# Attention beside an FFT filter: the PV product with V as the stationary operand

## The chip, the cores and the metric

The kernel runs on one core of a Trainium2 chip, in one launch. The metric is the device time of one execution in microseconds. The core's engines are named as the profile names them: PE multiplies matrices (PEld is its loading of the stationary operand), ACT evaluates functions such as exp, DVE works on vectors, POOL sets and copies memory here, and SP issues transfers. PE writes into PSUM, which has eight banks of 128 partitions by 512 f32 columns; the other engines read PSUM and write SBUF. The clock that PE gets is granted by a throttle and stands in the profile.

## The reference

x is 2048 tokens by 448 numbers in bfloat16. Two branches are computed from it and mixed token by token with a gate. A is attention with 16 heads of 28 numbers, B is a filter in the two-dimensional frequency domain.

```python
def reference(A_x, A_wqkv, A_wo, B_x, B_w_r, B_w_i, gate_w):
    # A: q, k, v from x @ wqkv (16 heads of 28)
    scores = einsum("bhqd,bhkd->bhqk", q, k) * 28 ** -0.5
    p = softmax(scores)
    a = (einsum("bhqk,bhkd->bhqd", p, v)).reshape(1, 2048, 448) @ wo
    # B: filter of the same x
    X = rfft2(x, axes=(-2, -1)) * (w_r + 1j * w_i)
    b = irfft2(X, s=(2048, 448), axes=(-2, -1)).astype(bfloat16)
    g = sigmoid((x * gate_w).sum(-1, keepdims=True))
    return g * a + (1 - g) * b
```

## The kernel before

**Layout.** Everything lies in one class, and a scheduler orders the instructions of each engine by the priority at which they were written; what stands between `bg_begin` (L146) and `bg_end` gets a late priority and fills the gaps of the main loop. PSUM is shared out in four parts: `ps_S` (L164) has two buffers of three banks ("psS") for the scores, `ps_pv` (L167) one bank ("pv") for the weighted sums of V, and `ps_bg` (L170) one bank ("bg") for everything in the background.

**Start.** `phase_setup` (L230) issues one transfer of all of x (L236), then the weights, gate and output weights (L243 to L248), all from SP. It transposes x with 64 matmuls against the identity (L257) into xT, 128 features by 2048 tokens in four slices of features. The last slice has 64 rows only; the rows behind are set to zero by POOL (L265, and L267 for the weights) and row 64 to one, so that the weights can add a constant. `fft_setup` (L576) loads the constants of the filter at late priority. Then, for the head tile of the "rep" group and for tile 0, `proj_setup` (L304) copies the weights of each head to columns 32s+1 to 32s+28, and `proj_matmuls` (L337) makes q and k transposed, up to four heads in the four strips of 32 partitions. Row 0 of a strip carries a bias: one in k, and -(|q|^2 + max|k|^2)/2 in q, so that the exponent stays below zero. The norms are matmuls with the selector Sel4 (`proj_knorm`, L361, and `proj_qbias`, L393); the bias row is made in a small tile and moved into q by a transfer on SP. `vproj_and_gate` (L280) makes V for all tokens, 29 columns a head with a one at the end, and the gate.

**Main loop.** `main_loop_group` (L528) runs six groups. The first is one head, replicated in three strips, with its query chunks side by side; the other five hold three heads each. A chunk is up to three heads by 512 queries. For each of 16 key tiles, PE makes three score tiles of 128 keys by 512 queries in three row tiles (L553), ACT takes exp of all 1536 columns (L557) into one of three "Pt" buffers, and PE adds up P V with 12 matmuls (L562):

```python
nc.tensor.matmul(psPV[:, e, j, 0:Dh + 1],
                 lhsT=Pt[:, e, 128 * j:128 * j + 128],
                 rhs=self.vsb[:, i, h, 0:Dh + 1],
                 start=first, stop=last)
```

P is the stationary operand (a load of 128 x 128 for each matmul), V moves with 29 columns, and the result lies by tokens: column 28 of each head is the softmax's denominator. At a chunk's end DVE takes the reciprocal of the denominators, 128 x 12 (L568), and multiplies (L571) into osb, token-major.

**Background.** In this order: `proj_tile` (L426) for tiles 1 to 3; the filter as products with cosine and sine matrices in five steps, `fft_f1` (L605, four matmuls of 450 columns a token tile), `fft_f2` and `fft_f5` (both `_stage_A`, L617, 32 times two matmuls of 256 columns), `fft_f34` (L647, transposes, four matmuls, complex product on DVE) and `fft_f678` (L691); and `tail` (L721), which for each of 16 token tiles transposes osb (L733), copies it (L738, L740), multiplies with Wo (L747), mixes with the filter's result by the gate (L749, "fin") and sends it out (L751). The last four token tiles depend on the last chunk.

Of the kernel before, what the change touches and what calls it, by code (L numbers as in the profile page):

```python
# [16 lines left out]

BG_PRIORITY_BASE = 10_000_000


def bcast_last(ap: bass.AP, n: int) -> bass.AP:
    assert ap.ap[-1][1] == 1
    new_ap = [list(p) for p in ap.ap[:-1]] + [[0, n]]
    return bass.AP(tensor=ap.tensor, offset=ap.offset, ap=new_ap)


def strided_rows(t_ap: bass.AP, row0: int, stride: int, count: int) -> bass.AP:
    pstep = t_ap.ap[0][0]
    return _AP(tensor=t_ap.tensor, offset=t_ap.offset + row0 * pstep,
               ap=[[pstep * stride, count]] + [list(x) for x in t_ap.ap[1:]])  # L30

# [71 lines left out]
class Kernel:  # L103
    def __init__(self, tc, A_x, A_wqkv, A_wo, B_w_r, B_w_i, gate_w, out):
        self.tc = tc
        nc = self.nc = tc.nc
        self.A_x, self.A_wqkv, self.A_wo = A_x, A_wqkv, A_wo
        self.B_w_r, self.B_w_i, self.gate_w, self.out_ap = B_w_r, B_w_i, gate_w, out
        self.H = H = 16
        self.S = S = A_x.shape[1]  # L110
        self.D = D = A_x.shape[2]
        self.Dh = Dh = D // H
        self.SCALE = float(Dh) ** -0.5
        self.NT = NT = S // 128
        self.P = P = 128
        self.J = P // NT
        self.F = F = D // 2 + 1
        self.F2 = 2 * F
        self.dch = chunks_of(D, 128)
        self.NDC = len(self.dch)  # L120
        self.fch = chunks_of(F, 128)
        self.QW = 512
        assert Dh + 1 <= 32 and S % 512 == 0 and P % NT == 0 and NT <= P and H % 4 == 0
        self.x = A_x[0]
        self.outv = out[0].rearrange("(p t) d -> p t d", t=NT)
        self.tiles = [[(s, 4 * T + s) for s in range(4)] for T in range(H // 4)]
        lastT = len(self.tiles) - 1
        hl = H - 1
        self.tiles[lastT] = [(s, h) for (s, h) in self.tiles[lastT] if h != hl]
        self.tiles.append([(0, hl)])  # L130
        self.repT = len(self.tiles) - 1
        self.head_loc = {}
        for T, ent in enumerate(self.tiles[:-1]):
            for s, h in ent:
                self.head_loc[h] = (T, s)
        groups = [("rep", hl)]
        others = [h for h in range(H) if h != hl]
        for i in range(0, len(others), 3):
            groups.append(("tri", others[i:i + 3]))
        self.groups = groups  # L140
        self.NG = len(groups)
        self._bgcount = 0
        self._bg_saved = None
        self._evac_cnt = 0

    def bg_begin(self):  # L146
        assert self._bg_saved is None
        self._bg_saved = self.tc.cur_priority
        self.tc.cur_priority = BG_PRIORITY_BASE + self._bgcount

    def bg_end(self):
        assert self._bg_saved is not None
        self._bgcount = self.tc.cur_priority - BG_PRIORITY_BASE
        self.tc.cur_priority = self._bg_saved
        self._bg_saved = None

    def setup_pools(self, ctx):
        tc = self.tc
        self.per = ctx.enter_context(tc.tile_pool(name="per", bufs=1))
        self.rot2 = ctx.enter_context(tc.tile_pool(name="rot2", bufs=2))  # L160
        self.rot3 = ctx.enter_context(tc.tile_pool(name="rot3", bufs=3))
        self.ps = ctx.enter_context(tc.tile_pool(name="ps", bufs=2, space=bass.MemoryType.PSUM))
# [10 lines left out]
    def evac2(self, o, i):  # L173
        if self._evac_cnt % 2 == 0:
            self.nc.vector.tensor_copy(out=o, in_=i)
        else:
            self.nc.scalar.copy(out=o, in_=i)
        self._evac_cnt += 1

    def build(self):  # L180
        with ExitStack() as ctx:
            self.setup_pools(ctx)
            self.phase_setup()
            self.fft_setup()
            NTL = len(self.tiles)
            self.qTt = [None] * NTL
            self.kTt = [None] * NTL
            def full_proj(Tlist):
                for T in Tlist:
                    self.proj_setup(T)  # L190
                for which in ("q", "k"):
                    for T in Tlist:
                        self.proj_matmuls(T, which)
                for T in Tlist:
                    self.proj_knorm(T)
                for T in Tlist:
                    self.proj_qbias(T)
            full_proj([self.repT, 0])
            self.vproj_and_gate()
            bg_items = [("proj", T) for T in range(1, NTL - 1)]  # L200
            bg_items += [("fft", f) for f in
# [28 lines left out]
    def phase_setup(self):  # L230
# [45 lines left out]
        for s in range(4):  # L276
            nc.gpsimd.memset(self.Sel4[32 * s:32 * s + 32, s:s + 1], 1.0)
# [523 lines left out]
```

## Time and profile before

Three runs took 565.3 (the median), 585.66 and 563.74 us. One of them was taken again with the hardware profiler; the table is of that execution.

| | |
|---|---|
| span of the profiled execution | 564.9 us |
| PE / PEld busy | 508.8 (90%) / 256.5 (45%) |
| ACT busy | 490.0 (87%) |
| DVE busy | 213.8 (38%) |
| POOL busy | 20.8 (4%) |
| mean granted clock of PE | 0.805 |
| first exponential starts | 56.8 us |
| last exponential ends | 545.4 us |
| from there to the end | 19.5 us |

The page gives busy times by engine, then 40 slices of the span with the granted clock, the chain of work that ended last, and the costliest groups of instructions. In a group's line, "out<-in" are the program's tiles, then come partitions x elements, the count, the busy time and the mean of one in ns. In the timeline each line has start (us), duration, engine, source line, operation, tiles, shapes, the number of equal instructions run together, and in brackets the wait before and what ended it. A table by windows has, for each stretch, its length, then for PE, PEld, DVE, ACT and POOL the busy time and the number of instructions, then the granted clock, the share of the DMA engines and the number of executions.

### The profile page before, as it was taken

The numbers are of one execution on the slowest core, as the hardware profiler recorded it, in microseconds if no ns is written. First come the engines' busy times: TensorE is split into PE (matmuls) and PEld (weight loads), VectorE is DVE, ScalarE is ACT, GpSimd is POOL, SyncE is SP. The second block draws the span as 40 slices with busy tenths as digits, with TensorE's granted clock in tenths as the row PEclk, the third lists the DMA queues.
The fourth block names the chain that finished last, engine by engine and source line by source line (L and its number), as shares of the span: only waits on it lengthen the run. The fifth ranks groups of instructions, "written<-read, shape, count | busy, mean of one in ns | idle before, by whom it ended". The sixth has DMA issues, their size and how long they took to land.

```text
span 564.9 us, 13975 instructions
## 1 busy us (share of the span) xinstructions
PE 508.8 (90%) x6088; PEld 256.5 (45%) x6088; DVE 213.8 (38%) x633; ACT 490.0 (87%) x392; POOL 20.8 (4%) x92
## 2 busy tenths in 40 slices
PE   2979988999998899999899999999998998899986
PEld 2424432444443355544355555555544554445541
DVE  4573323322223533322556555333233233333343
ACT  2153986999999899999899999999999999999961
POOL 6240010000000000000000000000000000000000
PEclk9989985699999575799575555757799589999996
DMA  7300000000000000000012221000000000000111
GB/s 252 126 19 20 2 2 1 2 1 2 2 1 2 3 1 1 1 3 1 1 33 54 55 55 26 1 2 1 20 21 20 21 20 20 21 1 27 34 34 41
DMA packets 13947, 13.45 MB, mean 24 GB/s; under 512 B 6191, under 2 KB 12783, under 8 KB 13758
## 3 DMA queue, kind: packets, MB, share of 16 engines
q1 hardware_dynamic: 13886, 12.57, 7.8%
q8 instruction: 47, 0.77, 0.6%
q14 instruction: 14, 0.11, 0.1%
HBM read 10.14 MB, written 1.84 MB: 21 GB/s over the span
## 4 chain that ended last, share of the span: by engine, by line
ACT 48%; PE 39%; issue 7%; DVE 3%; DMA 1%; SPq 0%; ACTq 0%
ACT Pt L557 48%; PE psS L553 12%; PE psPV L562 9%; PE pv L290 2%; PE pqk L353 2%; PE psT L641 2%; DMA Wqkv_sb<-in_A_wqkv_dram 1%; PE psY L714 1%; PE pf_s L747 1%; PE ptx L257 1%; PE psB L662 1%; PE psA L623 1%; PE psZ L705 1%; DVE fin L749 1%; PE psB L664 1%
## 5 line engine op out<-in xcount | busy, mean ns | idle before, releaser
L557 ACT ACTIVATE Pt<-psS 128x1536 bf16<-128x1536 f32 (+1 forms) x352 | 469.4, 1460 | 19.4 <-PE psS L553 10.2
L562 PEld LDWEIGHTS <-Pt 128*128 128x128 bf16 x4096 | 142.3, 100 | 131.1 <-ACT Pt L557 109.6
L562 PE MATMUL psPV<-vsb,Pt 128*128 128x29 bf16 x4096 | 167.1, 182 | 25.3 <-ACT Pt L557 20.8
L553 PE MATMUL psS<-qTa_2343,kTa_2344 32*128 32x512 bf16 x256 | 69.3, 507 | 0.5 <-ACT Pt L557 0.5
L553 PE MATMUL psS<-qTa_950,kTa_951 32*128 32x512 bf16 x256 | 68.8, 530 | 0.4 <-ACT Pt L557 0.4
L553 PE MATMUL psS<-qTa_249,kTa_250 32*128 32x512 bf16 x256 | 60.6, 439 | 1.8 <-ACT Pt L557 1.8
L553 PE MATMUL psS<-qTa_3760,kTa_3761 32*128 32x512 bf16 x192 | 26.5, 384 | 0.5 <-ACT Pt L557 0.4
L718 DVE TENSOR_SCALAR bm_sb<-psY,omg 128x448 bf16<-128x448 f32 x16 | 10.9, 683 | 36.8 <-PE psY L714 36.8
L667 DVE CAST Xri<-psB 128x225 bf16<-128x225 f32 x16 | 6.3, 396 | 25.7 <-PE psB L665 25.7
L749 DVE SCALAR_TENSOR_TENSOR fin<-pf,gsb,bm_sb 128x448 bf16<-128x448 f32 x12 | 8.2, 684 | 20.7 <-PE pf L747 20.7
L257 PE MATMUL ptx<-ident,xtok 128*128 128x128 bf16 (+1 forms) x64 | 6.7, 287 | 10.3 <-DMA xtok<-in_A_x_dram 7.7
L553 PEld LDWEIGHTS <-kTa_250 32*128 32x128 bf16 x256 | 12.8, 93 | 6.4 <-issue 2.3
L747 PE MATMUL pf<-Wo_sb,oTt 128*128 128x448 bf16 (+1 forms) x48 | 14.8, 374 | 0.7 <-DVE oTt L740 0.7
L553 PE MATMUL psS<-qTa_207,kTa_208 32*128 32x512 bf16 x64 | 14.4, 420 | 0.6 <-ACT Pt L557 0.5
L553 PEld LDWEIGHTS <-kTa_951 32*128 32x128 bf16 x256 | 13.0, 97 | 4.1 <-issue 1.8
L553 PEld LDWEIGHTS <-kTa_2344 32*128 32x128 bf16 x256 | 13.0, 95 | 3.6 <-issue 1.2
L571 DVE TENSOR_TENSOR osb<-psPV,recip 128x112 bf16<-128x112 f32 x64 | 13.6, 266 | 0.6
L290 PE MATMUL pv<-Wqkv_sb,xT 128*128 128x449 bf16 x64 | 13.5, 372 | 0.0
L603 DVE CAST V_5523<-psA 97x256 bf16<-97x256 f32 x16 | 6.8, 424 | 16.4 <-PE psA L625 16.4
L603 DVE CAST U_192<-psA 128x256 bf16<-128x256 f32 x16 | 6.8, 425 | 15.7 <-PE psA L625 15.7
L623 PE MATMUL psA<-R_sb,X_sb 128*128 128x256 bf16 (+1 forms) x32 | 12.2, 383 | 0.0
L623 PE MATMUL psA<-R_sb,G_sb 128*128 128x256 bf16 (+1 forms) x32 | 12.2, 382 | 0.0
(484 smaller groups left out, 541.6 us busy)
## 6 DMA issues: line engine op xcount, KB each, us to landing
RBg<-cRB SPq DMA_DIRECT2D x16, 128.0 KB, 2.0
xtok<-in_A_x_dram SPq DMA_DIRECT2D x1, 1792.0 KB
out_dram<-fin SPq DMA_DIRECT2D x16, 112.0 KB, 1.7
CSg<-cCS SPq DMA_DIRECT2D x16, 96.0 KB, 1.8
Wqkv_sb<-in_A_wqkv_dram SPq DMA_DIRECT2D x3, 336.0 KB, 7.4
Wg<-in_B_w_r_dram SPq DMA_DIRECT2D x16, 56.2 KB, 1.8
Wg<-in_B_w_i_dram SPq DMA_DIRECT2D x16, 56.2 KB, 2.0
Bd_sb<-cBd SPq DMA_DIRECT2D x1, 450.0 KB, 3.8
```

What stands on the lines that cost most here:

```text
L257: nc.tensor.transpose(out=pt[0:dsz, k, :], in_=self.xtok[:, t, d0:d0 + dsz], identity=self.ident[:])
L290: nc.tensor.matmul(pv[:, e, 0:D + 1], lhsT=self.xT[:, c, 128 * t:128 * t + 128], rhs=self.Wqkv_sb[:, c, 2 * D:3 * D + 1], start=(c == 0), ...
L353: nc.tensor.matmul(pqk[0:M, e, :], lhsT=Wg[:, c, 0:M], rhs=self.xT[:, c, 512 * b:512 * b + 512], start=(c == 0), stop=(c == NDC - 1))
L553: nc.tensor.matmul(psS[:, e, :], lhsT=kTa[32 * s:32 * s + 32, 128 * i:128 * i + 128], rhs=qTa[32 * s:32 * s + 32, qs:qs + QW], start=True, ...
L557: nc.scalar.activation(out=Pt[:, 0:ne, :], in_=psS[:, 0:ne, :], func=ACT.Exp, scale=self.SCALE)
L562: nc.tensor.matmul(psPV[:, e, j, 0:Dh + 1], lhsT=Pt[:, e, 128 * j:128 * j + 128], rhs=self.vsb[:, i, h, 0:Dh + 1], start=first, stop=last)
L571: nc.vector.tensor_tensor(out=self.osb[:, t0:t0 + NQT, h * Dh:(h + 1) * Dh], in0=psPV[:, e, :, 0:Dh], in1=bcast_last(recip[:, e, :, 0:1], Dh),
L603: self.nc.vector.tensor_copy(out=o, in_=i)
L623: nc.tensor.matmul(ps[0:fn, :], lhsT=data_sb[:, t, fs:fs + fn], rhs=Rr, start=True, stop=False)
L641: nc.tensor.transpose(out=psT[:, ri * 256 + fs:ri * 256 + fs + fn], in_=U_tiles[fb][0:fn, ri, g, :], identity=self.ident[0:fn, 0:fn])
L747: nc.tensor.matmul(pf[:, 0:D], lhsT=oTt[0:dsz, c, :], rhs=self.Wo_sb[0:dsz, c, :], start=(c == 0), stop=(c == NDC - 1))
L749: nc.vector.scalar_tensor_tensor(out=fin[:], in0=pf[:, 0:D], scalar=self.gsb[:, t:t + 1], in1=self.bm_sb[:, t, :], op0=ALU.mult, op1=ALU.add)
```

## The change

The class is written anew. In **PV**, V becomes the stationary operand: a load of 128 keys by 32 columns, in column tile (0, 32j) for the head j of a tile of four; P moves with 512 columns, and the result is transposed, four heads in the four strips of 32 partitions of one bank. Row 0 of a strip is the denominator. The head's one stands in column 0 of a vsb that is 32 columns a head.

**One stream.** The groups go by query chunk b and head tile T: 16 groups of 16 key tiles by four heads, 1024 units of 128 keys by 512 queries, taken three at a time without regard to a group's end (341 steps of three and one of one). The scores of step s+1 are written before the sums of step s. Six Pt buffers instead of three. The replicated head goes.

**Normalising** happens at each of the 16 group ends: the bank is copied to SBUF, an f32 matmul with a selector spreads each denominator over its strip, DVE takes the reciprocal of 128 x 512 and multiplies into oT, which is transposed.

**Output** therefore needs no transposes: `out_block` multiplies slices of oT with a Wo that lies in four groups of strips. It runs in the stream, a token tile a step, once the filter is done.

**Prologue.** x comes in four blocks of 512 tokens on SP, the weights and the gate on ACT's queue. For each block come 16 transposes, the copies, and K of tile 0; Q of tile 0 for the first chunk only. V is made inside the stream, one block ahead of the unit that needs it, and the background is a generator, of which one item is taken a step: K and Q of the other tiles, then the filter as before. A group whose Q or K isn't there takes as many items as it needs at once. The biases: k gets its one by an addition of kone, the norms come through selN spread over rows, and q's bias is added by DVE, without a transfer. The clearing of vsb, now all of 128 x 8192, and of the constants is on POOL; the scheduler decides the order there.

```diff
-    def main_loop_group(self, g):
...
-                        nc.tensor.matmul(psPV[:, e, j, 0:Dh + 1],
-                                         lhsT=Pt[:, e, 128 * j:128 * j + 128],
-                                         rhs=self.vsb[:, i, h, 0:Dh + 1],
-                                         start=first, stop=last)
...
+        for b in range(self.NQ):
+            t0 = b * self.TPQ
+            nc.sync.dma_start(out=self.xtok[:, t0:t0 + self.TPQ, :], in_=self.xv[:, t0:t0 + self.TPQ, :])
+        for c, (d0, dsz) in enumerate(self.dch):
+            nc.scalar.dma_start(out=self.Wqkv_sb[0:dsz, c, 0:2 * D], in_=self.A_wqkv[d0:d0 + dsz, 0:2 * D])
...
+    def constants(self):
...
+            nc.gpsimd.memset(self.xT[lrows:P, lastc, :], 0.0)
+            nc.gpsimd.memset(self.Wqkv_sb[lrows:P, lastc, :], 0.0)
...
+            nc.gpsimd.memset(self.kone[r:r + 1, :], 1.0)
+        self.vsb = per.tile([P, NT, H, 32], BF16, name="vsb")
+        nc.gpsimd.memset(self.vsb[:], 0.0)
+        nc.gpsimd.memset(self.vsb[:, :, :, 0:1], 1.0)
...
+    def k_block(self, T, b, ps, first):
...
+        self.project(ps, self.wk, T, b)
+        sq = self.rot2.tile([P, QW], BF16, name="sq")
+        nc.vector.tensor_scalar(out=self.kT[T][:, cols], in0=ps, scalar1=self.kone[:, 0:1], scalar2=None,
+                                op0=ALU.add)
...
+    def k_norm(self, T, b, sq, kmin):
...
+        pn = self.ps_bg([P, QW], F32, name="pn")
+        nc.tensor.matmul(pn[:], lhsT=self.selN[:], rhs=sq[:], start=True, stop=True)
+        nc.vector.tensor_reduce(out=kmin[:, b:b + 1], in_=pn[:], axis=AX.X, op=ALU.min)
...
+    def q_bias(self, T, b, sq, pn):
...
+        nc.tensor.matmul(pn, lhsT=self.selN[:], rhs=sq[:], start=True, stop=True)
+        nc.vector.scalar_tensor_tensor(out=self.qT[T][:, cols], in0=pn, scalar=self.nhk[T][:, 0:1],
+                                       in1=self.qT[T][:, cols], op0=ALU.add, op1=ALU.add)
...
+    def prologue(self):
...
+        warm = self.per.tile([P, 1], F32, name="warm")
+        nc.scalar.activation(out=warm[:], in_=self.kone[:], func=ACT.Exp)
...
+        for b in range(self.NQ):
+            pt = self.ps_S([P, self.NDC, QW], BF16, name="pt")
...
+            nc.vector.tensor_copy(out=self.xT[:, 0:2, cols], in_=pt[:, 0:2, :])
+            nc.scalar.copy(out=self.xT[:, 2, cols], in_=pt[:, 2, :])
...
+            ps = self.ps_pv([P, QW], F32, name="pk")
+            sq = self.k_block(0, b, ps[:], True)
+            self.k_norm(0, b, sq, kmin)
+            if b == 0:
+                ps = self.ps_bg([P, QW], F32, name="pq")
+                qsq = self.q_block(0, 0, ps[:], True)
+        pn = self.ps_bg([P, QW], F32, name="pn")
+        self.q_bias(0, 0, qsq, pn[:])
...
+        nxt = qk(steps[0])
+        for s, step in enumerate(steps):
+            psS = nxt
+            ne = len(step)
+            Pt = self.per.tile([P, self.UNIT, QW], BF16, name="Pt", bufs=6)
+            nc.scalar.activation(out=Pt[:, 0:ne, :], in_=psS[:, 0:ne, :], func=ACT.Exp, scale=self.SCALE)
+            if s + 1 < len(steps):
+                nxt = qk(steps[s + 1])
+            for e, (g, i, j) in enumerate(step):
+                b, T = groups[g]
+                if g == 0 and vdone <= i:
+                    self.v_block(i)
+                    vdone = i + 1
...
+                nc.tensor.matmul(psPV[g][r:r + 32, :], lhsT=self.vsb[:, i, 4 * T + j, :], rhs=Pt[:, e, :],
+                                 start=(i == 0), stop=(i == NT - 1), tile_position=(0, r))
+                if i == NT - 1 and j == 3:
+                    self.normalise(psPV.pop(g), T, b)
...
+            if not done:
+                pull(1)
+            elif pend_out and s + 1 < len(steps):
+                self.out_block(*pend_out.pop(0), self.ps_bg)
...
+    def normalise(self, psPV, T, b):
...
+        nc.vector.tensor_copy(out=oU[:], in_=psPV[:])
+        pr = self.ps_pv([P, QW], F32, name="pr")
+        nc.tensor.matmul(pr[:], lhsT=self.selB[:], rhs=oU[:], start=True, stop=True)
+        rc = self.rot2.tile([P, QW], F32, name="rc")
+        nc.vector.reciprocal(out=rc[:], in_=pr[:])
+        nc.vector.tensor_tensor(out=self.oT[T][:, QW * b:QW * (b + 1)], in0=oU[:], in1=rc[:], op=ALU.mult)
+
+    def out_block(self, b, k, pool):
...
+        for T in range(self.NTL):
+            nc.tensor.matmul(pf[:, 0:D], lhsT=self.oT[T][:, 128 * t:128 * (t + 1)], rhs=self.Wo_sb[:, T, :],
+                             start=(T == 0), stop=(T == self.NTL - 1))
```

## The prediction

> **What bounds the kernel now.** I read the page first (busy shares, slices, chain), then single steps in the timeline, then windows of equal granted clock.
>
> ```profile
> PE 508.8 (90%) x6088; PEld 256.5 (45%) x6088; DVE 213.8 (38%) x633; ACT 490.0 (87%) x392; POOL 20.8 (4%) x92
> ...
> PEclk9989985699999575799575555757799589999996
> ...
> ACT 48%; PE 39%; issue 7%; DVE 3%; DMA 1%; SPq 0%; ACTq 0%
> ...
> L557 ACT ACTIVATE Pt<-psS 128x1536 bf16<-128x1536 f32 (+1 forms) x352 | 469.4, 1460 | 19.4 <-PE psS L553 10.2
> ```
>
> ACT's exponentials carry the middle: 352 of them. Starts of back-to-back 1536-wide ones lie 1.33 us apart (more than half of all spacings), so 336 x 1.33 + 16 x 0.5 = 455 us is their floor. The first starts at 56.8, the last ends at 545.4: 488.6 us, so 33 us of waits. Before it lie 56.8 us of loads and projections, after it 19.5 us of output.
>
> ```profile
> 55.20 1.03 PE L474 MATMUL pqk_952<-xT,WaugQ_902 128*128 128x512 bf16 x4
> 56.27 0.69 DVE L478 CAST qTa_950<-pqk_952 128x512 bf16<-128x512 f32 x1
> 56.81 2.79 ACT L557 ACTIVATE Pt<-psS 128x1536 bf16<-128x1536 f32 x2 [0.23 <-PE psS L553]
> 57.01 1.02 PE L474 MATMUL pqk_958<-xT,WaugQ_902 128*128 128x512 bf16 x4
> ```
>
> This is the first exponential and, around it, the one-bank "bg" pool at work: four matmuls, DVE's copy, and only then the next four. One such item holds the bank 57.01 - 55.20 = 1.81 us, more than an exponential.
>
> ```profile
> 110.28 0.46 PEld L562 LDWEIGHTS <-Pt 128*128 128x128 bf16 x12 [0.17 <-ACT Pt L557]
> ...
> 110.77 0.39 PE L553 MATMUL psS<-qTa_249,kTa_250 32*128 32x512 bf16 x3
> 111.09 0.11 PEld L612 LDWEIGHTS <-xT 128*128 128x128 bf16 x2 [0.23 <-issue]
> ```
>
> A step at full clock: 12 PV matmuls 0.49, three QK matmuls side by side in row tiles 0.32, then background. At half clock QK takes 0.54 (102.39 less 101.85), PV stays near 0.5.
>
> ```profile
> 82.00:106.00 24.00, 21.71 (x182) 7.77 (x182) 8.22 (x15) 18.40 (x20) 0.00 (x0) 0.50 0.00 1
> 110.00:154.00 44.00, 40.63 (x555) 19.16 (x554) 10.32 (x22) 44.00 (x34) 0.00 (x0) 1.00 0.01 1
> 208.00:228.00 20.00, 20.00 (x226) 10.99 (x227) 6.39 (x17) 19.41 (x15) 0.00 (x0) 0.50 0.00 1
> ```
>
> The clock (third number from the end) is 0.50 where little runs beside attention (82 to 106) or only stage A (208 to 228), and 1.00 beside the dense 450-column matmuls of f1 (110 to 154). In stage A at half clock the exponentials lie 1.46 apart.
>
> **The change, part by part.** Durations are of this profiled execution. Its span, 564.9, is 0.4 us from the median of the runs, 565.3, so I sum to a span and call that the time.
>
> 1. *Exponentials.* 1024 units by threes: 341 x 1.33 + 0.6 = **454.1 us** at best.
>
> 2. *Start.* Before the first exponential now stand only x, K of tile 0, one Q block. But POOL's order in the built program puts kone behind a chain, and kT's first eviction on DVE and the last x copies on ACT (behind "warm") wait for kone. The chain: the clearing of Wqkv_sb's spare rows waits for the gate DMA, which ACT issues behind the weights; x and weights are 1792 + 1176 KB at the 252 GB/s of slice 1, so it lands near 12 us. Then that memset 1.2 (L267), the selectors 1.0, vsb's memset of 8192 columns at 0.88 ns (1.80 us for 2048):
>
> ```profile
> 1.00 1.80 POOL L265 MEMSET xT<- 64x2048 bf16 x1
> ```
>
> 7.2, eight small ones 0.8: kone at 22.2. From there one pk bank, one bg bank: x copies and first square 2.0 and norm 0.4; three K rounds of 1.03 + 0.69 + 0.58 + 0.37 + 0.2 = 2.9, 8.6; Q with eviction and square between them 1.75; last reduce 0.8; bias 0.37 + 0.74; QK 0.6. Sum 15.3. First exponential at **37.5** instead of 56.8. Bounds 27 (memset nearly free, gate early) and 42 (these matmuls at half clock).
>
> 3. *PV.* 4096 small matmuls become 1024 of 512 columns in column tiles. No row shows a column tile. Below: the QK triple, 0.32 (0.54 at half clock). Above: three in series, 3 x 0.229 (L353: 12 in 2.75) + 0.1 = 0.79. I take 0.32, since QK is the nearest row: same columns, a quarter of the array, three at once. A step without background is then 0.32 + 0.32 = 0.64, hidden under 1.33.
>
> The step now switches shape three times instead of twice. The row: after QK the next weights wait 0.23 at full clock, 0.44 at half, and this lies inside my 0.32 and 0.54. The Trainium skill, "TensorEngine Tiling (Array Packing)", section Key Properties, says that a change of tiling mode drains the engine, which speaks against the change; with one more 0.23 a step would be 0.87, still hidden where nothing runs beside it, and f1 and the projections would add some 10 us to my sum. The page "TensorE: Matmul & The Clock Gate", Part 3, gives 2.38x for three column tiles, which no row here can show; by it the triple is an estimated 0.29.
>
> 4. *V and the projections inside the stream, through one bank.* The PE order has all 16 V blocks and 20 of the 54 K/Q items before the 29th exponential. Bank times: V 0.92 + 0.62 (1.04 ns a column from the evictions of 512 and 1536) + glog 0.1 + 0.1 = 1.73; K or Q 1.81; norm or bias 0.37 + 0.67 + 0.1 = 1.14. So 16 x 1.73 + 10 x 1.81 + 10 x 1.14 + 2 for norms that also wait for their square = 59, against 29 x 1.33 = 38.6: **+20.4**. PE is in order, so QK stands behind each wait. In the next 34 items K and norm follow each other: 1.03 + 0.69 + square 0.35 (1.21 for 2048) + 0.14, then 1.14, 3.3 a pair and 2.66 for two exponentials: 17 x 0.64 = **+10.9**. f1: 0.92 + 0.63 + 0.09 = 1.64 a step, 16 x 0.31 = **+5**.
>
> 5. *FFT.* Stage A (56 steps): at full clock 0.64 + 0.45, hidden; at half 0.54 + 0.54 + 0.5 = 1.58. I take half of them at half clock: 28 x 0.25 = **+7**. f34: copy, matmul, copy, six products 2.85 a pair, 16 x 0.19 = **+3**. f678: 4.8 of PE and 4.3 of bank in 5.3: 0.
>
> 6. *Steps with nothing beside them,* about 82 at the end: two steps cost (exponential 1.45 + 0.17 + PV 0.54 + QK 0.61 + 0.2) = 2.97 at half clock, 1.485 each: 82 x 0.155 = **+12.7**; nothing at full clock. The same sum for stage A before gives 1.43, measured 1.46.
>
> 7. *Normalising, 16 times.* Copy 0.69, an f32 matmul that no row shows (between 0.23 and 0.92; I take 0.9), then a reciprocal of 512 columns.
>
> ```profile
> L568 DVE RECIPROCAL recip<-psPV x22: 182/232/234, 79.0 to 545.9; 128x12 f32<-128x12 f32 x21, 128x4 f32<-128x4 f32 x1
> ```
>
> 4 columns take 182 ns, 12 take 232: 6.25 ns each, 3.36 us for 512; not below 0.69 (a plain read), and I take 3.36. The next group's PV stands behind it (one pv bank). The program puts four QK triples ahead of that PV, so ACT goes on: from the last exponential of a group, 0.6 + 0.69 + 1.0 + 3.5 and then 9 to 13 PVs give 7.7 where 6.9 was due, and QK behind the f32 matmul loses 0.25: 1.1 at full clock, 3.3 at half. The first group has all six Pt buffers full: +5. The second stalls the bank queue: +3.5. Nine at 1.1, four late ones at 3.3: **+31.6** in all.
>
> 8. *Tail.* PV 0.5, copy 0.75, f32 matmul 1.1, reciprocal 3.4, product 0.6, projection 0.6, four fin of 0.68 one after another 2.8, and 2.7 from the last fin's end to the span's end as now; with clock and waits **14** instead of 19.5. The transposes and oTt copies that it replaces go.
>
> Sum: 37.5 + 454.1 + 20.4 + 10.9 + 5 + 7 + 3 + 12.7 + 31.6 + 14 = **596 us**. What hides each free edit is ACT; POOL's weight copies for tiles 1 to 3 lie before first use.
>
> **Rivals.**
> *Full clock, cheap reciprocal (not slower).* Its place is the light steps: if the 512-column PV keeps the grant at 1.00, parts 5 (7) and 6 (12.7) go and the late boundaries fall by 9: 567, within 2%. It decides from the point where PE's work without background counts as busy: for it speaks 1.00 beside f1; against, 0.50 in 82 to 106, and PV plus QK fill less of a step than now. With the reciprocal at its lower bound, another 22 go: 545, faster.
> *Column tiles in series.* PV 0.79: A +8, f34 and f678 +27, f1 and projections +18 with their waits, 12 in the light steps as now, but the clock rises: less 14, and so about 638. For it: no row shows column tiles. Against: QK's three do run together.
> *The change does little*: the bank items lie in ACT's shadow, parts 4 gone, 560. Against it stands 1.81 measured.
>
> **Numbers.** Forecast 0.55 (570 to 620), full clock alone 0.14, with cheap reciprocal 0.09, no bank bound 0.07, series 0.15. Two per cent, 11 us, is about what a measurement tells from no change: faster by more 0.12, same 0.18, slower 0.70. Low 545 and high 645 take in the outer cases.
>
> **What will show it.** First exponential at 27 to 42; bank items 1.7 to 1.8 and exponentials over 1.6 apart in the first 64 steps; PV triples 0.3 to 0.4; reciprocal near 3.4; clock 0.5 in the last third with spacing near 1.49. Wrong if the PV triple takes 0.7, if the spacing is 1.33 from the start, or the clock stays at 1.00.

## The result, and the profile after

The changed kernel takes **667.4 us** (median of four runs, 657.7 to 670.2); the kernel before took 574.3 beside it. The ratio is **1.173, interval 1.137 to 1.210**: slower, by more than the range of the prediction allowed (545 to 645). The kernel before ran between 563 and 591 us in all runs of this study, a spread that goes with its granted clock (0.805 at a span of 564.9, 0.744 at 584.5), so a single run is read beside its stages.

The page of the changed kernel: busy times, the granted clock in 40 slices, the chain that ended last, and the groups that matter.

```profile
span 665.3 us, 7367 instructions
PE 552.2 (83%) x2934; PEld 171.5 (26%) x2944; DVE 260.6 (39%) x476; ACT 486.4 (73%) x358; POOL 18.3 (3%) x38
...
PEclk9669888799999898695565555899986565555556
...
PE 51%; ACT 26%; DVE 15%; issue 4%; DMA 2%; POOL 1%; ACTq 0%; DVEq 0%; POOLq 0%
...
L378 ACT ACTIVATE Pt<-psS 128x1536 bf16<-128x1536 f32 x342 | 477.8, 1451 | 132.1 <-PE psS L368 93.5
L389 PE MATMUL psPV<-Pt,vsb 128*32 128x512 bf16 x1024 | 177.5, 500 | 48.9 <-ACT Pt L378 28.8
...
L411 DVE RECIPROCAL rc<-pr 128x512 f32<-128x512 f32 x16 | 53.7, 3357 | 18.4 <-PE pr L409 18.4
```

ACT has lost the chain: 48% of it before, 26% now, and ACT stands idle for 132 us ahead of its exponentials, 93.5 of them until PE has the scores. PE has half as many instructions and more busy time. DVE, 3% of the chain before, holds 15%, and one group stands out: 16 reciprocals of 3.36 us.

The first exponential starts at 40.6, the last ends at 649.4, the tail is 15.9. Between them lie 341 spacings of exponentials. Their floor, 341 x 1.33, is 453.5; what each stage loses over it is the sum of its spacings less 1.33 each:

| steps | forecast | measured | without the division (experiment 1) |
|---|---|---|---|
| 0 to 28: V, K, Q | 25.4 | 44.0 | 34.5 |
| 28 to 64: K, Q | 14.4 | 15.2 | 15.6 |
| 64 to 81: f1 | 6.1 | 6.6 | 5.9 |
| 81 to 232: stage A, f34, stage A, f678 | 17.7 | **64.3** | 12.2 |
| 232 to 341: attention and output | 27.0 | 24.7 | 18.4 |
| sum | 90.6 | 154.8 | 86.6 |

(The forecast's group ends are shared out to the stages in which they lie.) 46.6 of the 64.2 us missed are in the filter's steps, 18.6 in the first 28. The timeline at one group end in f34 (lines of weight loads, transfers and others left out):

```profile
294.90 5.48 ACT L378 ACTIVATE Pt<-psS 128x1536 bf16<-128x1536 f32 x4 [0.77 <-PE psS L368]
295.02 3.35 DVE L411 RECIPROCAL rc<-pr 128x512 f32<-128x512 f32 x1
295.27 0.26 PE L477 MATMUL psB<-UT,CSg 128*128 128x225 bf16 x1
296.40 0.40 PE L368 MATMUL psS<-qT_128,kT_132 32*128 32x512 bf16 x3 [0.88 <-ACT Pt L378]
297.75 0.39 PE L368 MATMUL psS<-qT_128,kT_132 32*128 32x512 bf16 x3 [0.95 <-ACT Pt L378]
298.29 0.57 DVE L479 CAST Xri<-psB 128x450 bf16<-128x450 f32 x1
298.42 0.81 PE L389 MATMUL psPV<-Pt,vsb 128*32 128x512 bf16 x9 [0.28 <-DVE rc L411]
```

The filter's matmuls end at 295.5 and their bank waits for DVE's copy (Xri), which stands behind the reciprocal until 298.3; the next PV waits for it too. PE does two triples of scores in 2.9 us. ACT goes on meanwhile, as forecast. What was not forecast comes behind it. In the 3.41 us before 299.1 PE was busy for 1.47, and then the clock falls. In the table by windows (length, then PE, PEld, DVE, ACT, POOL, then the granted clock):

```profile
278.60:299.10 20.50, 16.51 (x139) 8.17 (x138) 17.72 (x54) 19.34 (x16) 0.00 (x0) 1.00 0.32 75
299.10:340.10 41.00, 40.98 (x175) 11.04 (x174) 16.78 (x50) 27.66 (x20) 0.00 (x0) 0.50 0.04 9
```

At 299.1 the clock falls to 0.50 and stays there for 41 us, with PE busy all the time and ACT 27.66 of 41. Before, the same stage ran at 1.00 with ACT 19.34 of 20.5. At full clock the filter's steps are hidden under the exponentials, at half clock PE sets the pace; 0.53 is the mean of the whole second stage A (312.6 to 366.4), where PE is busy 52.2 of 53.8 us.

### The profile page after: what moved, and what is told of

Its sections match the earlier page's. It is cut to its first block, busy times and chain, and to the rows that moved or that the text cites. A ratio compares the mean times of both kernels' runs of the same rounds, so it can differ in the third digit from the quotient of the medians.

```text
span 665.3 us, 7367 instructions
## 1 busy us (share of the span) xinstructions
PE 552.2 (83%) x2934; PEld 171.5 (26%) x2944; DVE 260.6 (39%) x476; ACT 486.4 (73%) x358; POOL 18.3 (3%) x38
## 4 chain that ended last, share of the span: by engine, by line
PE 51%; ACT 26%; DVE 15%; issue 4%; DMA 2%; POOL 1%; ACTq 0%; DVEq 0%; POOLq 0%
ACT Pt L378 25%; PE psPV L389 14%; PE psS L368 12%; DVE rc L411 7%; PE pr L409 3%; PE pk L217 3%; PE pq L217 2%; PE psA L444 2%; PE pvx L292 2%; PE psY L515 2%; PE pf L419 2%; PE psT L457 1%; DVE vsb L294 1%; PE psA L446 1%; PE psZ L506 1%
## 5 line engine op out<-in xcount | busy, mean ns | idle before, releaser
L378 ACT ACTIVATE Pt<-psS 128x1536 bf16<-128x1536 f32 x342 | 477.8, 1451 | 132.1 <-PE psS L368 93.5
L389 PE MATMUL psPV<-Pt,vsb 128*32 128x512 bf16 x1024 | 177.5, 500 | 48.9 <-ACT Pt L378 28.8
L389 PEld LDWEIGHTS <-vsb 128*32 128x32 bf16 x1024 | 49.6, 99 | 163.1 <-issue 148.3
L411 DVE RECIPROCAL rc<-pr 128x512 f32<-128x512 f32 x16 | 53.7, 3357 | 18.4 <-PE pr L409 18.4
L368 PE MATMUL psS<-qT_126,kT_130 32*128 32x512 bf16 x256 | 50.4, 494 | 7.1 <-ACT Pt L378 6.2
L368 PE MATMUL psS<-qT_128,kT_132 32*128 32x512 bf16 x256 | 50.6, 473 | 6.1 <-ACT Pt L378 6.0
L368 PE MATMUL psS<-qT_129,kT_133 32*128 32x512 bf16 x256 | 50.8, 513 | 4.6 <-ACT Pt L378 4.6
L368 PE MATMUL psS<-qT_127,kT_131 32*128 32x512 bf16 x256 | 46.7, 461 | 4.6 <-ACT Pt L378 4.6
L217 PE MATMUL pk<-xT,wk 128*128 128x512 bf16 x59 | 23.6, 523 | 5.8 <-DVE xT L275 5.1
L409 PE MATMUL pr<-oU,selB 128*128 128x512 f32 x32 | 24.4, 855 | 1.5 <-DVE oU L407 1.3
L368 PEld LDWEIGHTS <-kT_130 32*128 32x128 bf16 x256 | 10.4, 95 | 45.2 <-issue 44.4
L368 PEld LDWEIGHTS <-kT_131 32*128 32x128 bf16 x256 | 10.1, 94 | 38.5 <-issue 37.5
L217 PE MATMUL pq<-xT,wq 128*128 128x512 bf16 x59 | 18.0, 415 | 0.8 <-DVE qT_126 L258 0.5
L292 PE MATMUL pvx<-Wqkv_sb,xT 128*128 128x449 bf16 x64 | 15.8, 371 | 2.4 <-DVE kmin L238 1.4
L459 DVE COPY UT<-psT 128x450 bf16<-128x450 bf16 x32 | 12.5, 390 | 13.1 <-PE psT L457 13.0
```

The source lines that it names most:

```text
L217: self.nc.tensor.matmul(ps, lhsT=W[:, c, T, :, :].rearrange("p j d -> p (j d)"), rhs=self.xT[:, c, self.QW * b:self.QW * (b + 1)], start=( ...
L292: nc.tensor.matmul(pv[:, 0:D + 1], lhsT=self.xT[:, c, 128 * t:128 * (t + 1)], rhs=self.Wqkv_sb[:, c, 2 * D:3 * D + 1], start=(c == 0), sto ...
L368: nc.tensor.matmul(psS[:, e, :], lhsT=self.kT[T][r:r + 32, 128 * i:128 * (i + 1)], rhs=self.qT[T][r:r + 32, QW * b:QW * (b + 1)], start=Tr ...
L378: nc.scalar.activation(out=Pt[:, 0:ne, :], in_=psS[:, 0:ne, :], func=ACT.Exp, scale=self.SCALE)
L389: nc.tensor.matmul(psPV[g][r:r + 32, :], lhsT=self.vsb[:, i, 4 * T + j, :], rhs=Pt[:, e, :], start=(i == 0), stop=(i == NT - 1), tile_posi ...
L409: nc.tensor.matmul(pr[:], lhsT=self.selB[:], rhs=oU[:], start=True, stop=True)
```

## The experiments

All are edits of the changed kernel or of one another. "Filter" is the loss over the floor in steps 81 to 232 (64.3 in the changed kernel). Single runs are compared with 667.4; a difference of 13 us or less, the spread of the changed kernel's own runs, is not read. They ran on several chips, the kernel before spreads over 28 us in all its runs, and a single difference of 15 to 30 us is weak for that reason; it is read with the stages of its trace.

### 1. What of the division costs

**Without the division.**

```diff
-        nc.vector.tensor_copy(out=oU[:], in_=psPV[:])
-        nc.tensor.matmul(pr[:], lhsT=self.selB[:], rhs=oU[:], start=True, stop=True)
-        nc.vector.reciprocal(out=rc[:], in_=pr[:])
-        nc.vector.tensor_tensor(out=self.oT[T][:, QW * b:QW * (b + 1)], in0=oU[:], in1=rc[:], op=ALU.mult)
+        nc.vector.tensor_copy(out=self.oT[T][:, QW * b:QW * (b + 1)], in_=psPV[:])
```

> Left out: the division by the softmax's denominators. At a group's end DVE only copies the sums to oT (0.69 us), so that the f32 matmul, the reciprocal of 3.36 us and the product are gone, and the next group's PV waits 0.7 us for the bank instead of about 6. Theory A (the bank of the sums, held through the reciprocal, costs 3 to 5 us at most of the 16 group ends): 615 to 625 us, and the losses of the five last group ends, 21.8 us over the 1.33 floor, fall under 4. Rival (the time lost lies in the filter's steps at half clock, and the group ends only show it): 640 or more.

591.9 us: 75.5 less, more than theory A said. The filter loses 12.2 at a clock of 1.00 from 44 to 437 us, so the rival fell in its form; what it named, the half clock in the filter's steps, came with the division here. Of the gain 52.1 us lie in the filter's steps, 9.5 in the first 28, 6.3 in the last 109 and 6.0 in the tail. The other expectation, that the last five group ends lose under 4, was not met: the last stage still loses 18.4.

**The reciprocal off the bank of the sums.**

```diff
+        nc.vector.reciprocal(out=rc[:], in_=oU[:])          # in SBUF, at the group's end
...
+        pr = self.ps_bg([P, QW], F32, name="pr")            # four steps later
+        nc.tensor.matmul(pr[:], lhsT=self.selB[:], rhs=rc[:], start=True, stop=True)
+        nc.vector.tensor_tensor(out=self.oT[T][:, QW * b:QW * (b + 1)], in0=oU[:], in1=pr[:], op=ALU.mult)
```

> All is computed; the reciprocal stays as long (128 x 512) but is taken of the copy in SBUF, before the selector's matmul, so that the bank of the sums is free after the copy of 0.69 us; the matmul and the product follow four steps later through the background's bank. vsb is cleared to one instead of zero, so that no spare row is divided by zero. Theory A1 (the wait for the bank of the sums stops PE, and the clock falls with it): close to the run without the division, 592 to 612, clock over 0.82. Rival A2 (DVE's 3.36 us are what costs, since the background's one bank waits behind them): 635 to 655.

660.7: no gain that can be read, and outside both expected ranges. A1 fell. First stage A and f34 ran at 1.00 and lost 8.3, but then the clock fell again, and f678 lost 41.4:

```profile
340.80:468.70 127.90, 120.73 (x612) 37.17 (x610) 49.66 (x86) 92.48 (x65) 0.00 (x0) 0.74 0.05 15
```

**DVE's long instruction alone, and the f32 matmul alone.**

```diff
-        nc.vector.reciprocal(out=rc[:], in_=pr[:])
+        nc.vector.tensor_copy(out=rc[:], in_=pr[:])          # first run
...
-        self.selB = per.tile([P, P], F32, name="selB")
+        self.selB = per.tile([P, P], BF16, name="selB")      # second run, oU alike
```

> Left out: the reciprocal; DVE copies the spread denominators instead (128 x 512 from PSUM, 0.69 us for 3.36), so the result is not divided. All else, the f32 matmul, the bank, the product, stays. Theory A2 (the length of DVE's reciprocal makes the cost of the division): 600 to 615, near the run without any of it (591.9). Rival A3 (the f32 matmul on PE, 1 to 2 us at every group end, with the wait for it): 640 or more.

> The selector and the copied sums are bfloat16 instead of f32, so that the matmul that spreads the denominators takes 0.23 to 0.43 us instead of 0.9 to 2.1; the reciprocal of 3.36 us and the bank stay. Theory A3 (f32 matmul): 615 to 630. Rival A2 (DVE's reciprocal): 650 to 665. If neither this run nor the one with the copy gains much, the division costs as a chain of all its steps.

604.8 and 650.6. 62.7 of the 75.5 us go with DVE's 16 x 2.67 = 42.7 us; the bank is held, the f32 matmul is there, and all the filter runs at full clock. From f34 on ACT is busy 96% of the time:

```profile
240.80:420.90 180.10, 152.67 (x1141) 59.41 (x1140) 87.29 (x233) 173.66 (x128) 0.00 (x0) 1.00 0.10 27
```

The run with the f32 matmul shortened is 17 faster, little more than the spread.

**The same work in pieces.**

```diff
+            for due, _, _, oU, rc in pend_norm:              # one piece of 128 columns a step
+                k = s - (due - 6)
+                if 0 <= k < 4:
+                    nc.vector.reciprocal(out=rc[:, 128 * k:128 * (k + 1)], in_=oU[:, 128 * k:128 * (k + 1)])
```

> All is computed; the reciprocal is off the bank of the sums as in the run that gave 660.7, and split: four instructions of 128 columns (0.84 us by 6.56 ns a column) in four consecutive steps instead of one of 3.36; matmul and product two steps later. DVE's total work stays. Theory A2, sharpened (what costs is that one DVE instruction stands for 3.36 us in front of the background's evictions, so that PE stands, the clock window runs empty and the filter's steps stay at half clock): 600 to 620. Rival (DVE's total work or the f32 matmul): 645 or more.

627.3, 33 below the run with one piece off the bank, though the four pieces take more together (0.94 us each, not the 0.84 expected):

```profile
L397 DVE RECIPROCAL rc<-oU x64: 893/936/954, 111.3 to 614.1; 128x128 f32<-128x128 f32 x64
```

It missed the expected 600 to 620. The clock fell once in the filter, to 0.50 from 219.7 to 253.8, and stage A lost 18.8; f34, the second stage A and f678 ran at 1.00 and lost 20.4. So it is the length in one piece more than the total; section 4 has the same comparison once more. That what stands behind it on DVE is the background's eviction is read from the timeline: no run gave the background a second bank or another engine to empty it.

### 2. The clock

```diff
+            if n >= first:                                   # first = 0, or 81
+                nc.tensor.matmul(psS[:, 0, :], lhsT=self.xT[:, 0, 0:128], rhs=self.xT[:, 1, 0:QW],
+                                 start=True, stop=True)
             for e, (g, i, j) in enumerate(step):             # the scores of step n
```

In all steps:

> Nothing is left out; ahead of each step's scores PE multiplies once more 128 x 128 by 512 columns into a bank that the scores then overwrite (342 useless matmuls, 0.23 us at full clock, 0.43 at half). Theory C (the clock goes by how much of the array is streamed through: a step of row tiles and column tiles streams 384 + 384 full-array columns, stage A 512 more, and at half clock that keeps itself down): the clock rises from 0.75 to over 0.9, stage A, f34 and f678 lose under 20 us over the floor instead of 64, and the whole comes to 610 to 630 although PE has more to do. Rival (the clock goes by PE being busy, which it already is, or by something else): clock as before, the 126 half-clock steps of the filter 0.43 us longer, 700 to 720.

From step 81 on:

> The changed kernel with the useless dense matmul of 512 columns ahead of the scores from step 81 on, not before, so that V, K, Q and f1 are as they were. Theory C (from there on the clock, once a group's end has thrown it to half, can't come back by what row and column tiles stream): clock over 0.9 from step 81 on, 625 to 637 us, below the 642.7 of the run with the dense matmul in all steps. Rival (what that run gained came from the first 81 steps or from another chip): 650 or more.

642.7 at a clock of 0.96, and 653.9 at 0.91; neither reached what its theory said (610 to 630, 625 to 637). In the first, PE was given 342 matmuls more and the single run is faster by 25 us: what the clock brings exceeds what they cost. The filter lost 39.6 instead of 64.3 and the last 109 steps 14.4 instead of 24.7, while steps 28 to 81, which ran at 0.98 already, lost 37.5 instead of 21.8. Whether the clock goes by PE's busy time can't be told from this, since the matmuls fill PE too. The gain of the late variant's single run hardly exceeds the spread, and its clock fell at 300.3 with the matmul in every step.

With the reciprocal off the bank as well, and with all the repairs of section 3:

> The reciprocal off the bank of the sums, as in the run that gave 660.7, and the dense matmul from step 81 on. Theory A1 with C (the wait for the bank is gone there, and what kept the time was the clock, which fell to half in the second stage A and in f678): with the clock kept, both lose under 15 us over the floor instead of 53, and the whole comes to 600 to 615. Rival A2 (DVE's 3.36 us block the background whatever the clock): 630 or more, and f678 still over 25 us above the floor at full clock.

> V ahead of the stream, reciprocal off the bank, kone first (634.8 us together), with the dense matmul from step 81 on. Theory C: stage A, f34, f678 and the light steps lose 30 us over the floor instead of 91, the whole comes to 570 to 580. If the three repairs were held back by DVE and not by the clock: over 610.

639.1 and 608.8 (604.2 to 610.9), where theory C had said 600 to 615 and 570 to 580. In the first, at a clock of 1.00, the second stage A and f678 still lost 12.9 and 19.2:

```profile
305.20:355.30 50.10, 47.55 (x287) 17.08 (x284) 24.75 (x59) 39.56 (x29) 0.00 (x0) 1.00 0.03 7
355.30:461.00 105.70, 101.48 (x655) 36.06 (x653) 44.35 (x74) 90.44 (x66) 0.00 (x0) 1.00 0.06 18
```

PE is full there, with the extra matmul in it. So holding the clock by useless work does not give the loss back, and how much of the division's 62.7 us is the stall and how much the clock after it stays open between the two: by these single runs at least 20 of it is not DVE's own 42.7.

### 3. The start, and V

```diff
+        nc.gpsimd.memset(self.kone[:], 0.0)                  # first of all on POOL
+        for r in range(0, P, 32):
+            nc.gpsimd.memset(self.kone[r:r + 1, :], 1.0)
+        nc.gpsimd.memset(self.Wqkv_sb[self.dch[-1][1]:P, self.NDC - 1, :], 0.0)
```

> Only the order on POOL is changed: the column kone and the clearing of the weights' spare rows come first, ahead of all other clearing and of the gate's transfer. Theory (the start waits for kone at 21.9 us): the first exponential moves from 40.6 to 30 to 33 us, the whole by about 8, to 652 to 660. Rival (kone is not what comes last; the weights, which land near 12 us, and matmuls at half clock are): first exponential at 37 or later, the whole within 3 us of before.

First exponential at 34.5 (30 to 33 expected), whole 655.3. These first 6 us are what the order on POOL cost; the whole's gain is within the spread.

```diff
+        for t0 in range(0, NT, 3):                           # at the end of the prologue
+            pool = self.ps_S([P, 3, 512], F32, name="pvx")
+            for t in range(t0, min(t0 + 3, NT)):
+                self.v_block(t, pool[:, t - t0, :])          # evictions by DVE and ACT in turn
...
-                if g == 0 and vdone <= i:
-                    self.v_block(i)
```

> The 16 blocks of V are made ahead of the stream, three at a time in the scores' banks, their evictions shared by DVE and ACT; the stream holds no V any more. Theory B (one bank, through which 16 blocks of V and 20 items of K and Q pass in the first 28 steps): the first exponential moves from 40.6 to about 56, the first 28 steps fall from 81 us to about 42, the whole to 640. Rival (the first 28 steps are held by something that V doesn't cause, such as K and Q or the order on PE): first exponential 56, these steps still over 60 us, the whole 660 to 670.

633.6, 33.8 less. The first 28 steps took 49.0 instead of 81.3, and the first exponential moved only to 44.0: V's matmuls fell into the waits of the prologue, which was not expected. The order of V inside the stream cost what the forecast named, and more.

### 4. P stationary again, and the sums

```diff
-                nc.tensor.matmul(psPV[g][r:r + 32, :], lhsT=self.vsb[:, i, 4 * T + j, :], rhs=Pt[:, e, :], ...)
+                for k in range(4):
+                    nc.tensor.matmul(psPV[g][:, j, k, 0:1 + self.Dh], lhsT=Pt[:, e, 128 * k:128 * (k + 1)],
+                                     rhs=self.vsb[:, i, 4 * T + j, 0:1 + self.Dh], ...)
...
+        nc.vector.reciprocal(out=rc[:], in_=psPV[:, :, :, 0:1])     # 128 x 16
+        for j in range(4):
+            h = 4 * T + j
+            nc.vector.tensor_tensor(out=self.osb[:, 4 * b:4 * (b + 1), h * Dh:(h + 1) * Dh],
+                                    in0=psPV[:, j, :, 1:1 + Dh], in1=bcast_last(rc[:, j, :, 0:1], Dh), op=ALU.mult)
```

> One part undone: P is the stationary operand again (12 matmuls of 29 columns a step, result by tokens), the division is that of before (reciprocal of 128 x 16 and four products), and the output goes through transposes; stream, prologue, order of the background and banks stay those of the changed kernel. Theory A (the group ends cost by the long reciprocal): about 45 us come back at the group ends and 4 are lost at the end, 620 to 630. Rival (the column-tile PV saves PE time that the filter's steps need): the steps of K, Q, f1 and the filter get 0.1 to 0.2 us longer each, some 230 of them, and the whole stays at 655 to 670.

594.7: 72.8 less by undoing this one part, PV with its division, where 620 to 630 was expected, and within 3 us of the run without any division. The clock still falls in the filter's steps (about 0.8 in the first stage A and in f34), and they lose only 11.5. The reciprocal there, and no one waits for it:

```profile
L412 DVE RECIPROCAL rc<-psPV x16: 239/258/259, 107.5 to 579.0; 128x16 f32<-128x16 f32 x16
```

The repairs together, with V stationary and with P stationary:

> The changed kernel with V ahead of the stream, the reciprocal off the bank, kone first, and vsb's clearing on DVE. If the three costs are separate (33.8 us for V by its run, 55 to 75 for the bank, 8 for kone), 550 to 570 us, no slower than the kernel before. If they hide one another, above 590.

> P as the stationary operand again with the short division (594.7 us in its own run), V ahead of the stream, kone first, vsb's clearing on DVE. By the sum of the single runs 594.7 - 33.8 - 8 = 553 us, faster than the kernel before and within 10 us of the sum with V stationary. If the column-tile PV is worth its PE time once the other costs are gone, this kernel is 10 us or more behind that one.

634.8 and 567.4, single runs both. With V stationary they are worth no more than V first alone (633.6); the single gains, 33.8, 12 and 6.7, would have given 615, and the clock fell to 0.65 in the first stage A. With P stationary they gave 27 of the 42 us that the single runs had named.

```diff
+                if s % 5 != 4:
+                    pull(1)                                  # background in four of five steps
...
+            b, k = divmod(g2, self.TPQ)                      # in f678: output as soon as filtered
+            if b in self.normed:
+                for _ in self.out_block(b, k, self.ps_bg):
+                    yield
```

> P stationary, V ahead of the stream, kone first (567.4 us), and the background taken in four of five steps instead of in all, each output block as soon as its token tile is filtered. Theory (K, Q and the 12 output blocks in a row lose 30 us over the floor because one bank and a half-clock PE get more than a step's worth, while 109 steps at the end get nothing): 540 to 552, faster than the kernel before. Rival (K and Q are needed when they are, and the spread takes nothing off): 563 or more.

> V stationary in column tiles, with all repairs: V ahead of the stream, kone first, the background in four of five steps, and a short division: the denominators of a group go by transfers on SP into 128 x 16, the reciprocal takes 0.25 us, transfers bring it back, and matmul and product follow eight steps later. If the column tiles are as good as P stationary once the long reciprocal is gone, within 8 us of that kernel, 545 to 560; if the f32 matmul and the half clock still tell, 575 or more.

P stationary: **550.6 us (548.2 to 552.5), 0.968 of the kernel before, 0.956 to 0.979**: within the expected 540 to 552, and faster than the kernel before and the changed one. Its page:

```profile
PE 489.1 (89%) x6028; PEld 252.5 (46%) x6048; DVE 209.3 (38%) x533; ACT 483.9 (88%) x366; POOL 10.5 (2%) x36
...
PEclk9998999999999777879867797599955595875555
```

V stationary with the denominators moved by transfers: 629.2 (619.8 to 637.7), 1.097 of before (1.064 to 1.129). No instruction on DVE is long there, and yet the filter lost 47.4: the clock fell at 194.2 behind steps without background, after 3.40 us in which PE was busy for 1.81. The pace makes such steps, but no run with V stationary has the short division without the pace, so that the pace is the cause isn't shown. What half clock then costs shows in two windows with background (not the same items), V stationary first, P stationary second:

```profile
194.20:235.20 41.00, 39.85 (x176) 9.69 (x173) 9.49 (x21) 32.35 (x23) 0.00 (x0) 0.50 0.01 1
```

```profile
395.90:440.30 44.40, 44.10 (x473) 21.57 (x473) 10.35 (x26) 39.50 (x29) 0.00 (x0) 0.50 0.07 21
```

41.0/23 = 1.78 us an exponential against 44.4/29 = 1.53. Last, the split reciprocal with V first and kone first:

> The split reciprocal with V ahead of the stream, kone first and vsb's clearing on DVE: V stationary with all its costs repaired but the last. By the sum of single runs (33.8 and 12 off the split run) 560 to 575, between the kernel before and the best with P stationary (550.6). If the column tiles themselves cost at half clock (one more change of shape a step), 590 or more.

581.3 (577.6 to 586.5), 1.025 of before (1.015 to 1.035), 6 us past the expected range and not as slow as 590. From the run at 634.8 it differs in the split alone (matmul and product come two steps later with it): 53 us, and the filter lost 18.7 instead of 71.9, at a clock of 1.00 instead of 0.76. With every cost but the last repaired, V as the stationary operand is no better than the kernel before, 14 us behind the single run of P stationary with the same repairs (567.4) and about 30 behind the one with the pace (550.6); both ran on other chips.

The dense matmul on the P-stationary sum, from step 225 on:

> P stationary, short division, V ahead of the stream, kone first (567.4 us), with the dense matmul from step 225 on, where only attention and the output's projection are left. The 18.6 us over the floor there lie in the output blocks at half clock (3.2 us a step instead of 1.33); at full clock 8 or less, so 553 to 558 us, 0.95 to 0.98 of the kernel before. Rival (the matmul costs as much as the clock brings): 565 or more.

592.0 (588.6 to 595.9) instead of 567.4, as the rival said. The matmul stands in the stream from 378.2 us on. The clock was 1.00 until 431.8, fell there with the matmul in every step (PE was busy for 2.41 of the 3.40 us before), and stayed at 0.50 to the end:

```profile
440.00:560.00 120.00, 113.00 (x1181) 40.77 (x1182) 6.24 (x22) 103.25 (x73) 0.00 (x0) 0.50 0.01 4
```

With V stationary, in the run at 639.1, the clock had stood at 1.00 with the same matmul from step 81 to 625.7 us. Here the matmul neither kept a high grant nor brought it back.

## Why the prediction was wrong

The direction held. The **step that failed is part 7**, normalising: 31.6 us forecast, 75.5 by the single run that leaves it out (6 of them in the tail, which part 8 had priced). The duration was right (3.36 taken, 3.357 measured), and so was ACT's delay where nothing stands beside it (3.3 forecast for a late group end, 2.9 measured at steps 277 and 298). Wrong was what waits for it. Part 7 named the next group's PV, behind the one bank of the sums; freeing that bank changed nothing that can be read. It counted DVE's queue once ("the second stalls the bank queue: +3.5") and left it out at the other ends, although part 4 had worked out that the background goes through one bank which DVE empties. At every group end with background a 3.36 us instruction stands in front of that eviction. And the clock was treated as given by the stage. The rows shown (0.50 beside stage A, 1.00 beside f1) did not say that the same stage can hold either. In the changed kernel the clock falls four times in the filter's steps, at 227.4, 261.6, 299.1 and 343.5, each time 3 to 5 us after a long reciprocal began and after 3.41 us in which PE was busy for 1.13, 1.71, 1.47 and 1.81. Without the division, and with the copy in the reciprocal's place, it did not fall between 46 and 437 us. A long reciprocal is not the only way to a fall, as section 4 shows.

**Part 5**, the filter, was 10 where 64.3 was measured, but it was right for what it priced: without the division the filter loses 12.2. The half of stage A at half clock came as nearly all of the second one (0.53; 1.00 without the division), and where the steps follow undisturbed their spacing is 1.63 to 1.68, not 1.58.

**Part 4** forecast 20.4 (25.4 with the first group's end) for the first 28 steps; 44.0 were measured. Its mechanism is in the trace: the exponential waits for PV, which stands behind V's eviction and holds a Pt buffer.

```profile
68.58 0.92 PE L292 MATMUL pvx<-Wqkv_sb,xT 128*128 128x449 bf16 x4
69.55 0.63 DVE L294 CAST vsb<-pvx 128x448 bf16<-128x448 f32 x1 [0.82 <-PE pvx L292]
70.23 0.47 PE L389 MATMUL psPV<-Pt,vsb 128*32 128x512 bf16 x3 [0.72 <-DVE glog L295]
70.79 1.45 ACT L378 ACTIVATE Pt<-psS 128x1536 bf16<-128x1536 f32 x1 [2.75 <-PE psPV L389]
```

This term was mis-sized, and 9.5 of the 44.0 went with the division: a V item holds the bank for 2.0 us, not 1.73, and a K or Q item 2.3 to 2.9, not 1.81, since on PE sums and scores stand between one item and the next. For K and Q afterwards 14.4 was forecast and 15.2 measured, for f1 6.1 and 6.6. The first agreement is in part luck: these steps lose 15.6 without the division too, so the items cost more than the forecast 10.9 and the 3.5 that part 7 added there did not come.

**Part 2** gave the first exponential at 37.5; it came at 40.6. kone was forecast for 22.2:

```profile
21.90 0.09 POOL L195 MEMSET kone<- 1x1 f32 x1
22.03 0.75 DVE L226 TENSOR_SCALAR kT_130<-pk,kone 128x512 bf16<-128x512 f32 x1 [1.72 <-POOL kone L195]
```

From there 18.7 us instead of 15.3: the page's clock is 0.6 in those slices, the bound that the part named. **Part 8**: 15.9 against 14.

**Part 6**, the steps with nothing beside them: 1.485 us forecast at half clock, 1.35 and 1.42 in turn measured, so the 58 such steps away from a group's end lose 2.9 us where the forecast gives them 9.

**Part 3** held: a PV triple in column tiles takes 0.32 at full clock and 0.54 at half, as the scores do, and the rival of column tiles in series fell. What it left aside is the third change of shape, for which the Trainium skill, "TensorEngine Tiling (Array Packing)", section Key Properties, had spoken. Stage A at half clock, before and after (weight loads; the bracket is the wait):

```profile
214.80 0.16 PEld L623 LDWEIGHTS <-X_sb 128*97 128x97 bf16 x1 [0.44 <-issue]
215.08 0.59 PEld L562 LDWEIGHTS <-Pt 128*128 128x128 bf16 x12
215.71 0.10 PEld L553 LDWEIGHTS <-kTa_250 32*128 32x128 bf16 x1
216.25 0.10 PEld L623 LDWEIGHTS <-X_sb 128*128 128x128 bf16 x1 [0.44 <-issue]
```

```profile
314.02 0.16 PEld L444 LDWEIGHTS <-G_sb 128*97 128x97 bf16 x1 [0.44 <-issue]
314.62 0.11 PEld L389 LDWEIGHTS <-vsb 128*32 128x32 bf16 x3 [0.35 <-issue]
315.16 0.10 PEld L368 LDWEIGHTS <-kT_132 32*128 32x128 bf16 x3 [0.44 <-issue]
315.70 0.11 PEld L444 LDWEIGHTS <-G_sb 128*128 128x128 bf16 x1 [0.44 <-issue]
```

With P stationary, PV has the shape of the filter's matmuls and its loads follow at once; one wait shows, and the period is 1.45 us. In column tiles a wait shows at each of three changes, and the period is 1.68. Hidden at full clock, this is 0.2 us a step at half. That page's rule agrees with the rows after; in the rows before, the change from PV to scores (215.71) shows no wait.

The rival that came nearest was column tiles in series (about 638, though its terms add up to 635), and by luck: it names another reason. The range ended at 645 because no rival joined the long reciprocal to the background's bank.

## What to carry to other kernels

A long instruction on an engine that empties other stages' buffers is priced by what stands behind it in that engine's queue at every place where it occurs, not only by who waits for its result; splitting it into pieces between the others' work gave back 33 us of 62.7 here, and 53 with the other repairs in. A layout that is cheap for the product can be dear for what follows: dividing along the free axis cost 128 x 512 in place of 128 x 16, and undoing PV with its division brought 72.8 us. Moving work ahead of a stream, into waits that exist, and spreading the rest over the steps that have room took P stationary from 594.7 to 550.6 (kone first included); the new product brought nothing over it.

## What the runs showed of the hardware

- The granted clock has two states in the same stage. The second stage A ran at 1.00 without the long reciprocal (289.1 to 326.4, ACT busy throughout) and at 0.53 with it. The Trainium skill, "TensorE: Matmul & The Clock Gate", Part 1, gives an idle window of about 3.4 us for the fall and a busy one of the same length for the rise. The shortest stretches here are 3.41 us, which agrees. But PE was not idle for that long before the fall at 299.1 (busy for 1.47 of 3.41 us, 0.95 the longest gap), and it was busy for 40.98 of 41.0 us afterwards without a rise.
- A useless dense matmul a step raised the mean clock from 0.75 to 0.96 and made the kernel 25 us faster (a single run). With P stationary the clock fell with the matmul in every step, at 431.8, and stayed at 0.50 for 160 us. Row and column tiles use a quarter of the array each; whether the grant goes by the share of the array in use, no run here shows.
- A reciprocal's cost is 6.56 ns a column at 512 columns (3.357 us) and 7.3 at 128 (0.936 us).
